# First four feature tiles of a mixture-of-experts layer in plain fp32, with three weight low parts moved to VectorE

## The chip, the cores and the metric

The kernel runs on one core of one Trainium2 chip. The metric is the device time of one execution in microseconds (us), median of several runs. TensorE is called PE, VectorE DVE, ScalarE ACT, GpSimd POOL and SyncE SP, as the profile does.

## The reference

Three layers run one after the other, all in fp32. An mLSTM layer over 2 batches, 8 heads, 768 steps and head size 40 gives a matrix x of 1536 tokens by 320. A dense mixture of 8 experts with Sinkhorn weights follows, and a top-1 mixture of 8 experts closes the program.

```python
h = np.maximum(x @ w1[e], 0.0)      # 320 -> 1024
ye = h @ w2[e]                      # 1024 -> 320
out += P[:, e:e + 1] * ye           # first mixture, all experts
out[mask] = gate_w[mask, None] * ye # second mixture, tokens of expert e
```

## The kernel before, in words

Tokens are worked in 12 tiles of 128. The tiles alternate between the two batches, so tiles 0 and 1 are the first chunks of both, tiles 2 and 3 the second, and so on. `lead` (line 304) computes attention for tiles 0 and 1 at once; `attn` (line 404) is a generator that does one later tile in some fifteen steps.

A product of two fp32 matrices is mostly done in the one-pass type fp32r. Each operand is split into a high part (ACT copies it to fp32r) and a low part (an engine subtracts the high part from the raw value), and three products are added: high by high, high by low, low by high. Contraction runs over the 320 features of x in three blocks of 128, 128 and 64; the third block holds high and low rows of x side by side, so two products do there. That makes 8 matmuls of 256 columns for one feature tile of 128 and two token tiles (`s1_unit`, line 844, matmuls at line 855). Behind them ACT writes the ReLU's high part `hh` (line 856) and DVE its low part `hl` (line 857). `transpose_x` (line 468) turns a token tile of x and splits it into `xh` and `xl`. `split_chunk` (line 597) splits one raw piece of a weight matrix: ACT casts at line 613, DVE or POOL subtracts at line 619, and then the next raw piece is loaded into the freed one of four buffers (`load_chunk`, line 576). The first expert's w1 comes in three raw pieces, its w2 in three more.

The first mixture is a list of items (line 554): tiles 0 and 1 with expert 0, tiles 2 and 3 with expert 0, then four tiles at a time. An item runs 8 feature tiles (stage 1), then for each token tile four pieces of six matmuls with w2 (stage 2, lines 861 to 863). Two background ticks, numbered u, stand in each feature tile and one behind each stage 2 piece. `bg_early` (line 1578) hangs attention work on them: the tables RT, AT, GT and DT (lines 1569 to 1572) say at which u a tile's decay rows R are made (line 207), its attention starts, and gate and decay chains start. So the order in which every engine sees its work is the order of this program text; each engine takes its queue strictly in that order.

At the end of `lead` the queues stand as follows. PE: values of tiles 0 and 1 (line 262), outer product 0 (line 267), transposes of x 0 (lines 473 and 474), two filler matmuls (line 192), transposes of x 1, outer product 1, then feature tile 0. POOL subtracts the low parts of the first two w1 pieces between its gate steps (lines 366 and 382), DVE that of the third (line 388). DVE also normalises tiles 0 and 1 (lines 272 to 274, 377) and scans the next gate chunk (lines 147 to 164).

Of the kernel before, what the change touches and what calls it, by code (L numbers as in the profile page):

```python
# [12 lines left out]
ALU = mybir.AluOpType  # L13
# [5 lines left out]
def mlstm_moe_moe_kernel(ctx, tc, q, k, v, i_gate, f_gate, o_gate, wg1, w1a, w2a, wg2, w1b, w2b, out):  # L19
# [169 lines left out]
    def keep_warm(n, cols=512):  # L189

        for _ in range(n):
            pe.matmul(warm_p[:, 0:cols], warm[:, 0:128], warm[:, 0:cols], start=True, stop=True)
# [111 lines left out]
    def lead(g1):  # L304
# [58 lines left out]
        for i in range(2):  # L363
            for a in range(2):
                values(pn[i], W[i], i, a)
        low = split_chunk(pool, wait=True)
        low()
        pc = [pst(), None]
# [12 lines left out]
        next(g1)  # L381
        low = split_chunk(pool, wait=True)
        low()
        transpose_x(xs_[0], 0, pst, act)
        next(g1)
        next(g1)
        keep_warm(2)
        low = split_chunk(wait=True)
        transpose_x(xs_[1], 1, ps1, act)
        pc[1] = pst()  # L390
        outer(pc[1], 1)
        low()
        next(g1)
        emit_const1()
# [92 lines left out]


    NBLK = 3
    TPB = NT // NBLK  # L490
# [77 lines left out]
    for n, (_, _, e) in enumerate(ITEMS):  # L568
        if n == 0 or ITEMS[n - 1][2] != e:
            chunks += [(e, "w7", t) for t in range(4)] if seven(n) else [(e, "w1", t) for t in range(3)]  # L570
            chunks += [(e, "w2", t) for t in range(3)]
    raws = {}
    nload = [0]
    nsplit = [0]

    def load_chunk():
# [13 lines left out]
        else:  # L590
            k0, k1 = 3 * t, min(3 * t + 3, NF)
            sp.dma_start(out=r[:, 0:(k1 - k0) * DM].rearrange("p (k d) -> p k d", d=DM),
                         in_=w2a[e, k0 * 128:k1 * 128, :].rearrange("(k p) d -> p k d", p=128))
        raws[n] = r
        nload[0] += 1

    def split_chunk(eng=None, wait=False, hi=None):
# [19 lines left out]

        def low():
            eng.tensor_tensor(out=l, in0=rv, in1=f32(h), op=ALU.subtract)  # L619
            load_chunk()  # L620
        if wait:
# [254 lines left out]
    def moe1(bg):  # L876
# [44 lines left out]
        for n, (t0, nt, e) in enumerate(ITEMS):  # L921
# [21 lines left out]
            else:  # L943
                assert not left_over
                for ft in range(NF):
                    s1_unit(t0, nt, ft, lambda: bg(n, 2 * ft))
                    if newe and (ft < 3 if n < EARLY - 2 else ft in (0, 2, 4)) or n == 0 and ft in (2, 4, 6):
                        split_chunk()
                    if sums is not None and ft > 3:
                        next(sums, None)  # L950
                        next(sums, None)
                    bg(n, 2 * ft + 1)
# [595 lines left out]
    with tc.manual_schedule():  # L1548
# [19 lines left out]

        RT = {3: 2, 6: 3, 17: 4, 27: 5, 37: 6, 47: 7, 55: 8, 63: 9, 71: 10, 79: 11}
        AT = {5: 2, 8: 3, 20: 4, 30: 5, 40: 6, 50: 7, 58: 8, 66: 9, 74: 10, 82: 11}  # L1570
        GT = {6: 2, 26: 3, 43: 4, 59: 5}
        DT = {5: 1, 20: 2, 36: 3, 54: 4, 70: 5}
        OT = {10: 2, 25: 4, 43: 6, 60: 8, 76: 10}
# [141 lines left out]
```

## Time and profile before

| what | value |
|---|---|
| median of 3 runs | 959.27 us (958.46 to 960.22) |
| profiled execution | 958.19 us, span 956.5 us |
| PE busy | 927.4 us, 97% of the span |
| DVE busy | 628.3 us, 66% |
| ACT busy | 442.2 us, 46% |
| POOL busy | 257.5 us, 27% |
| mean granted PE clock | 0.991 of full |

The span is the part of the profiled execution between its first and last recorded work. An engine's busy time is the union of its instructions; an idle gap carries the name of what ended it. A row of the timeline gives start, duration, engine, source line and operation, and in square brackets the idle time ahead of it with its releaser. In a view that merges instructions, a duration is that of the whole group. Lines are those of the kernel before. An fp32 matmul shows as two records in the trace, an fp32r matmul as one.

### The profile page before, as it was taken

Reading aid. Unit: us, or ns where it says so; the run is one execution under the profiler, and the core shown is the slowest. Engines: PE = TensorE matmul, PEld = TensorE weight load, DVE = VectorE, ACT = ScalarE, POOL = GpSimd, SP = SyncE. Lnnn points to the kernel's source line nnn. Section 1 sums busy time; section 2 is a strip of 40 time slices with the busy share of each in tenths; the row PEclk is TensorE's granted clock in tenths of the full one; section 3 lists DMA queues with packets and bytes.
Section 4 is the critical chain, followed back from the end, with each engine's and each line's share of the span. In section 5 each row is a group of like instructions: output and inputs, shape, how many; then the busy total and the mean of one; then the engine's idle time right before and its main releaser. Section 6 shows DMA issues by size and latency. Waiting matters only on the chain.

```text
span 956.5 us, 15330 instructions
## 1 busy us (share of the span) xinstructions
PE 927.4 (97%) x5714; PEld 833.7 (87%) x5714; DVE 628.3 (66%) x1325; ACT 442.2 (46%) x790; POOL 257.5 (27%) x271
## 2 busy tenths in 40 slices
PE   8999999999999999999999999999999999899995
PEld 5888888888999998999998889999988987678995
DVE  8767865667766877474856748484536469864772
ACT  4545635343445565352535436253332135565672
POOL 6313321001006341415051231402221102325411
PEclk9999999999999999999999999999999999999998
DMA  9824430323234103021210203022280034677540
GB/s 194 190 43 94 112 92 23 100 77 110 83 96 133 57 1 116 17 77 56 77 56 25 92 17 107 26 77 65 68 320 29 19 93 137 206 226 209 160 119 19
DMA packets 93711, 91.28 MB, mean 95 GB/s; under 512 B 54845, under 2 KB 82495, under 8 KB 93632
## 3 DMA queue, kind: packets, MB, share of 16 engines
q1 hardware_dynamic: 91424, 83.50, 30.8%
q0 software_dynamic: 2208, 6.75, 2.2%
q8 instruction: 47, 0.77, 0.3%
q14 instruction: 32, 0.26, 0.1%
HBM read 86.29 MB, written 4.76 MB: 95 GB/s over the span
## 4 chain that ended last, share of the span: by engine, by line
PE 84%; DVE 8%; DMA 2%; ACT 2%; issue 2%; POOL 1%; SPq 0%; POOLq 0%; DVEq 0%; ACTq 0%
PE a L750 17%; PE s L855 12%; PE s L861 8%; PE s L863 8%; PE s L862 8%; PE s L1414 3%; PE a L861 3%; PE a L863 3%; PE a L862 3%; PE s L750 3%; PE a L262 2%; PE s L1352 2%; PE a L252 1%; PE s L1387 1%; PE s L1397 1%
## 5 line engine op out<-in xcount | busy, mean ns | idle before, releaser
L861 PE MATMUL s<-w2h,hh 128*128 128x320 f32 x544 | 171.5, 315 | 0.0
L863 PE MATMUL s<-w2h,hl 128*128 128x320 f32 x544 | 168.2, 309 | 0.0
L862 PE MATMUL s<-w2l,hh 128*128 128x320 f32 x544 | 168.0, 309 | 0.0
L855 PE MATMUL s<-xh,w 128*128 128x512 f32 (+1 forms) x528 | 147.7, 379 | 2.3 <-DVE hl L857 1.7
L855 PEld LDWEIGHTS s<-xh,w 128*128 128x128 f32 x528 | 96.7, 191 | 22.7 <-DVE hl L857 4.1
L619 POOL TENSOR_TENSOR w2l<-raw,w2h 128x960 fp32r<-128x960 f32 (+1 forms) x24 | 50.1, 2098 | 228.8 <-ACT w2h L613 228.6
L861 PEld LDWEIGHTS s<-w2h,hh 128*128 128x128 f32 x544 | 102.3, 188 | 2.0
L862 PEld LDWEIGHTS s<-w2l,hh 128*128 128x128 f32 x544 | 102.4, 188 | 1.6
L863 PEld LDWEIGHTS s<-w2h,hl 128*128 128x128 f32 x544 | 102.1, 188 | 0.1
L856 ACT ACTIVATE hh<-s 128x512 fp32r<-128x512 f32 (+1 forms) x88 | 49.2, 559 | 107.2 <-PE s L855 107.2
L857 DVE SCALAR_TENSOR_TENSOR hl<-s,hh 128x512 fp32r<-128x512 f32 (+1 forms) x88 | 56.3, 640 | 58.5 <-ACT hh L856 58.3
L750 PE MATMUL a<-th,w 128*128 128x512 f32 (+1 forms) x224 | 80.5, 366 | 0.0
L750 PE MATMUL a<-ts,wx 96*128 96x512 f32 (+1 forms) x192 | 70.7, 368 | 0.9 <-DVE wx L732 0.9
L855 PE MATMUL s<-xl,w 128*128 128x512 f32 (+1 forms) x176 | 67.7, 385 | 1.7 <-DVE xl L483 1.7
L861 PE MATMUL a<-w2h,hh 128*128 128x320 f32 x224 | 69.3, 309 | 0.0
L863 PE MATMUL a<-w2h,hl 128*128 128x320 f32 x224 | 69.2, 309 | 0.0
L862 PE MATMUL a<-w2l,hh 128*128 128x320 f32 x224 | 69.1, 309 | 0.0
L889 DVE SCALAR_TENSOR_TENSOR acc<-s,probs,acc 128x320 f32<-128x320 f32 x68 | 37.3, 548 | 41.2 <-PE s L863 40.8
L777 DVE SCALAR_TENSOR_TENSOR hl<-s,hh 128x512 fp32r<-128x512 f32 (+1 forms) x64 | 39.6, 619 | 30.0 <-ACT hh L773 30.0
L785 ACT COPY pu<-a 128x512 f32<-128x512 f32 (+1 forms) x32 | 17.1, 534 | 87.9 <-PE a L750 82.5
L773 ACT ACTIVATE hh<-a 128x512 fp32r<-128x512 f32 (+1 forms) x64 | 35.0, 547 | 36.9 <-DVE a L780 34.3
L777 DVE SCALAR_TENSOR_TENSOR hl<-a,hh 128x512 fp32r<-128x512 f32 (+1 forms) x64 | 39.9, 623 | 15.1 <-ACT hh L773 12.4
(377 smaller groups left out, 2192.0 us busy)
## 6 DMA issues: line engine op xcount, KB each, us to landing
raw<-in_moe_w_dram SPq DMA_DIRECT2D x30, 512.0 KB, 3.8
raw<-in_moe_w_dram SPq DMA_DIRECT2D x30, 480.0 KB, 3.6
raw<-in_moe_w_dram SPq DMA_DIRECT2D x39, 320.0 KB, 4.3
raw<-in_moe_w_dram SPq DMA_DIRECT2D x40, 256.0 KB, 4.3
wr<-in_moe_w_dram SPq DMA_DIRECT2D x8, 1024.0 KB, 13.7
w2raw<-in_moe_w_dram SPq DMA_DIRECT2D x12, 640.0 KB, 4.1
raw<-in_moe_w_dram SPq DMA_DIRECT2D x42, 128.0 KB, 2.6
q<-in_q_dram SPq DMA_DIRECT2D x12, 160.0 KB, 3.6
```

The costliest lines, as they stand in the source:

```text
L619: eng.tensor_tensor(out=l, in0=rv, in1=f32(h), op=ALU.subtract)
L750: pe.matmul(bank, w, x, start=(first and n == 0), stop=(n == 3), skip_group_check=True)
L773: act.activation(out=hh[:, f, c], in_=p, func=AF.Relu)
L777: dve.scalar_tensor_tensor(out=hl[:, f, c], in0=p, scalar=0.0, in1=f32(hh[:, f, c]), op0=ALU.max, op1=ALU.subtract)
L855: pe.matmul(p, w[:, k, fs], x_[:, k, cols], start=(m == 0), stop=(m == len(mm) - 1))
L856: act.activation(out=hh[:, ft, 0:n], in_=p, func=AF.Relu)
L857: dve.scalar_tensor_tensor(out=hl[:, ft, 0:n], in0=p, scalar=0.0, in1=f32(hh[:, ft, 0:n]), op0=ALU.max, op1=ALU.subtract)
L861: pe.matmul(p[:, 0:DM], hh[:, f, c], w2h[:, w[n], :], start=(first and n == 0), stop=False)
L862: pe.matmul(p[:, 0:DM], hh[:, f, c], w2l[:, w[n], :], start=False, stop=False)
L863: pe.matmul(p[:, 0:DM], hl[:, f, c], w2h[:, w[n], :], start=False, stop=(last and n == len(cuts) - 1))
L889: dve.scalar_tensor_tensor(out=acc[:, tt, 0:DM], in0=p[:, 0:DM], scalar=probs[:, tt, e:e + 1], in1=acc[:, tt, 0:DM], op0=ALU.mult, op1=ALU ...
L1414: pe.matmul(p, a[:, k, fs], b[:, k, xs], start=(k == 0 and n == 0), stop=(k == 2 and n == 1))
```

## The change

The first four feature tiles of the first item (`plain_unit`) multiply the raw fp32 pieces of w1 with an unsplit fp32 copy of x, `xf`, in three plain fp32 matmuls of 256 columns each. `turn_x` only transposes x and copies it to `xf` on ACT; `split_x` makes `xh` and `xl` for both tiles behind feature tile 0. The low parts of all three w1 pieces are subtracted on DVE: two at the end of `lead`, the third behind feature tile 1. The raw pieces are read until feature tile 3, so the next three loads are issued behind it. The splits of the three w2 pieces move from feature tiles 2, 4, 6 to 4, 6, 7. In the background tables the rows R of tiles 2 and 3 move from u 3 and 6 to 5 and 7, their attention from 5 and 8 to 7 and 9, and one gate and one decay chain by two.

```diff
-        low = split_chunk(pool, wait=True)
-        low()
+        lows = [split_chunk(wait=True) for _ in range(2)]
         pc = [pst(), None]
         outer(pc[0], 0)
...
-        low = split_chunk(pool, wait=True)
-        low()
-        transpose_x(xs_[0], 0, pst, act)
+        turn_x(xs_[0], 0, pst)
+        keep_warm(2)
+        turn_x(xs_[1], 1, ps1)
+        pc[1] = pst()
+        outer(pc[1], 1)
+        lows.append(split_chunk(wait=True))
+        lows[0](False)
+        lows[1](False)
         next(g1)
         next(g1)
-        keep_warm(2)
-        low = split_chunk(wait=True)
-        transpose_x(xs_[1], 1, ps1, act)
-        pc[1] = pst()
-        outer(pc[1], 1)
-        low()
-        next(g1)
+        steps.extend([split_x, lambda: lows[2](False)])
         emit_const1()
...
+    xf = scr[:, 0:3 * 2 * L].rearrange("p (a t) -> p a t", t=2 * L)
+    steps = []
+    def turn_x(x, slot, ps):
+        px = ps()
+        for t in range(2):
+            pe.transpose(px[:, t * L:(t + 1) * L], x[:, t * L:(t + 1) * L], ident)
+        pe.transpose(px[0:64, 2 * L:3 * L], x[:, 256:DM], ident)
+        cols = slice(slot * L, (slot + 1) * L)
+        pv = px[:, 0:3 * L].rearrange("p (a t) -> p a t", t=L)
+        act.copy(out=xf[:, 0:2, cols], in_=pv[:, 0:2, :])
+        act.copy(out=xf[0:64, 2, cols], in_=pv[0:64, 2, :])
+    def split_x():
+        c = slice(0, 2 * L)
+        act.copy(out=xh[0][:, 0:2, c], in_=xf[:, 0:2])
+        act.copy(out=xh[0][0:64, 2, c], in_=xf[0:64, 2])
+        dve.tensor_tensor(out=xl[0][:, :, c], in0=xf[:, 0:2], in1=f32(xh[0][:, 0:2, c]), op=ALU.subtract)
+        dve.tensor_tensor(out=xh[0][64:128, 2, c], in0=xf[0:64, 2], in1=f32(xh[0][0:64, 2, c]), op=ALU.subtract)
+    def plain_unit(ft, w, mid):
+        p = ps1()[:, 0:2 * L]
+        for k in range(3):
+            r = slice(0, 128 if k < 2 else 64)
+            pe.matmul(p, w[k][r, ft * 128:(ft + 1) * 128], xf[r, k], start=(k == 0), stop=(k == 2))
+            if k == 0:
+                mid()
+        act.activation(out=hh[:, ft, 0:2 * L], in_=p, func=AF.Relu)
+        dve.scalar_tensor_tensor(out=hl[:, ft, 0:2 * L], in0=p, scalar=0.0, in1=f32(hh[:, ft, 0:2 * L]), op0=ALU.max, op1=ALU.subtract)
+        if steps:
+            steps.pop(0)()
+        if ft == PLAIN - 1:
+            for _ in range(3):
+                load_chunk()
...
-                    s1_unit(t0, nt, ft, lambda: bg(n, 2 * ft))
-                    if newe and (ft < 3 if n < EARLY - 2 else ft in (0, 2, 4)) or n == 0 and ft in (2, 4, 6):
+                    if n == 0 and ft < PLAIN:
+                        plain_unit(ft, first_raws, lambda: bg(n, 2 * ft))
+                    else:
+                        s1_unit(t0, nt, ft, lambda: bg(n, 2 * ft))
+                    if newe and (ft < 3 if n < EARLY - 2 else ft in (0, 2, 4)) or n == 0 and ft in (4, 6, 7):
                         split_chunk()
...
-        RT = {3: 2, 6: 3, 17: 4, 27: 5, 37: 6, 47: 7, 55: 8, 63: 9, 71: 10, 79: 11}
-        AT = {5: 2, 8: 3, 20: 4, 30: 5, 40: 6, 50: 7, 58: 8, 66: 9, 74: 10, 82: 11}
-        GT = {6: 2, 26: 3, 43: 4, 59: 5}
-        DT = {5: 1, 20: 2, 36: 3, 54: 4, 70: 5}
+        RT = {5: 2, 7: 3, 17: 4, 27: 5, 37: 6, 47: 7, 55: 8, 63: 9, 71: 10, 79: 11}
+        AT = {7: 2, 9: 3, 20: 4, 30: 5, 40: 6, 50: 7, 58: 8, 66: 9, 74: 10, 82: 11}
+        GT = {8: 2, 26: 3, 43: 4, 59: 5}
+        DT = {7: 1, 20: 2, 36: 3, 54: 4, 70: 5}
```

With the change, the low part stands at line 659, the plain matmuls at 514, hl of the plain feature tiles at 518, stage 1 at 896 to 898, stage 2 at 902 to 904, and the decay matmuls of `attn` at 412.

The first place is PE's queue from the end of `lead` into the item. In the names, s_384 and s_373 are the banks of x 1, s_414 and s_401 that of feature tile 0, w_81 is w1, and acc holds `xf` (its other end holds the gate chains). Before:

```order
L474 MATMUL s_384<-ident,x 64x128
L267 MATMUL a<-v_99,ku_97 128x82 x4
L855 MATMUL s_414<-xh_65,w_81 128x256
L855 MATMUL s_414<-xl_68,w_81 128x256
L855 MATMUL s_414<-xh_65,w_81 128x256 x2
L855 MATMUL s_414<-xl_68,w_81 128x256
L855 MATMUL s_414<-xh_65,w_81 128x256 x3
```

Two more feature tiles of the same form follow there, and then the two decay matmuls of tile 2 (line 414). The same place with the change:

```order
L495 MATMUL s_373<-ident,x 64x128
L267 MATMUL a<-v_99,ku_97 128x82 x4
L514 MATMUL s_401<-acc,raw 128x256 x3
L514 MATMUL s_416<-acc,raw 128x256 x3
L514 MATMUL s_423<-acc,raw 128x256 x3
L514 MATMUL s_435<-acc,raw 128x256 x3
L412 MATMUL a<-R,gl__109 128x512 x2
L896 MATMUL s_469<-xh_65,w_81 128x256
```

Four feature tiles now stand ahead of the decay matmuls instead of three, and none of them reads a split operand.

The second place is DVE's queue from the next gate chunk to the rows R of tile 2. Before:

```order
L153 TENSOR_TENSOR acc<-acc 16x128
L155 SCALAR_TENSOR_TENSOR acc<-msk,acc 16x128
L483 TENSOR_TENSOR xl_68<-s_384,xh_65 128x2x128
L484 TENSOR_TENSOR xh_65<-s_384,xh_65 64x128
L619 TENSOR_TENSOR w_81<-raw,w_81 128x1024
L157 CAST gx<-acc 16x128
L162 TENSOR_TENSOR gx<-acc,gx 16x128
L857 SCALAR_TENSOR_TENSOR hl<-s_414,hh 128x256
L164 TENSOR_TENSOR gl__109<-acc,gl__109 16x128
L857 SCALAR_TENSOR_TENSOR hl<-s_428,hh 128x256
L207 TENSOR_TENSOR R<-gx,mask 128x512 x2
```

With the change (one more hl, of s_423, and then R follow the last row):

```order
L659 TENSOR_TENSOR w_81<-raw,w_81 128x1024 x2
L153 TENSOR_TENSOR acc<-acc 16x128
L155 SCALAR_TENSOR_TENSOR acc<-msk,acc 16x128
L157 CAST gx<-acc 16x128
L518 SCALAR_TENSOR_TENSOR hl<-s_401,hh 128x256
L506 TENSOR_TENSOR xl_68<-acc,xh_65 128x2x256
L507 TENSOR_TENSOR xh_65<-acc,xh_65 64x256
L162 TENSOR_TENSOR gx<-acc,gx 16x128
L164 TENSOR_TENSOR gl__109<-acc,gl__109 16x128
L518 SCALAR_TENSOR_TENSOR hl<-s_416,hh 128x256
L659 TENSOR_TENSOR w_81<-raw,w_81 128x1024
```

The split of x moved behind the first hl and is done once for both tiles; two low parts of w1 joined this queue.

The third place is DVE's queue at the end of stage 1, where the scores of tiles 2 and 3 are weighed (line 257, each twice) and the last w2 pieces are split. Before:

```order
L857 SCALAR_TENSOR_TENSOR hl<-s_507,hh 128x256
L619 TENSOR_TENSOR w2l<-raw,w2h 128x960
L153 TENSOR_TENSOR acc<-acc 16x128
L155 SCALAR_TENSOR_TENSOR acc<-msk,acc 16x128
L857 SCALAR_TENSOR_TENSOR hl<-s_568,hh 128x256
L257 TENSOR_TENSOR W<-a,W 128x4x128 x2
L157 CAST gx<-acc 16x128
L857 SCALAR_TENSOR_TENSOR hl<-s_603,hh 128x256
L619 TENSOR_TENSOR w2l<-raw,w2h 128x640
```

With the change:

```order
L898 SCALAR_TENSOR_TENSOR hl<-s_519,hh 128x256
L153 TENSOR_TENSOR acc<-acc 16x128
L155 SCALAR_TENSOR_TENSOR acc<-msk,acc 16x128
L898 SCALAR_TENSOR_TENSOR hl<-s_561,hh 128x256
L659 TENSOR_TENSOR w2l<-raw,w2h 128x960
L257 TENSOR_TENSOR W<-a,W 128x4x128 x2
L157 CAST gx<-acc 16x128
L257 TENSOR_TENSOR W<-a,W 128x4x128 x2
L898 SCALAR_TENSOR_TENSOR hl<-s_597,hh 128x256
```

The weighing of tile 2 now stands behind hl of feature tile 6 (s_561) and the low part of the second w2 piece; before, it stood behind hl of feature tile 5 (s_568). On PE the values of tile 2, which read the weighed scores, moved from feature tile 7 to between the first pieces of stage 2.

## Rows read from the trace of the kernel before

**Rows 1.** The page: PE's busy time, and PE over 40 slices of the span.
```profile
PE 927.4 (97%) x5714; PEld 833.7 (87%) x5714; DVE 628.3 (66%) x1325; ACT 442.2 (46%) x790; POOL 257.5 (27%) x271
...
PE   8999999999999999999999999999999999899995
```

**Rows 2.** The timeline of PE, 17 to 30 us: start, duration, instructions, idle time ahead.
```profile
17.89 0.66 PE L473 MATMUL a<-ident,x 128*128 128x128 f32 x2 [1.10 <-DVE num L374]
...
23.55 0.39 PE L855 MATMUL s<-xl,w 128*128 128x256 f32 x1 [1.73 <-DVE xl L483]
...
25.13 0.80 PE L855 MATMUL s<-xh,w 128*128 128x256 f32 x2 [0.59 <-DVE w L619]
...
29.04 1.01 PE L414 MATMUL a<-R,gl__109 128*128 128x512 f32 x2 [0.31 <-DVE R L207]
```

**Rows 3.** The timeline of DVE, 14 to 30 us.
```profile
14.77 2.01 DVE L272 SCALAR_TENSOR_TENSOR den<-num 128x8 f32<-128x8 f32 x1
...
18.14 0.17 DVE L272 SCALAR_TENSOR_TENSOR den<-num 128x8 f32<-128x8 f32 x1
...
18.78 0.49 DVE L377 TENSOR_TENSOR x<-num,den 128x320 f32<-128x320 f32 x1
...
19.90 0.41 DVE L483 TENSOR_TENSOR xl<-a,xh 128x256 fp32r<-128x256 f32 x1
...
20.64 2.10 DVE L153 TENSOR_TENSOR acc<-acc 16x128 f32<-16x128 f32 x1
...
23.85 1.23 DVE L619 TENSOR_TENSOR w<-raw,w 128x1024 fp32r<-128x1024 f32 x1
24.99 0.21 DVE L157 CAST gx<-acc 16x128 fp32r<-16x128 f32 x1
...
28.21 1.28 DVE L207 TENSOR_TENSOR R<-gx,mask 128x512 fp32r<-128x512 f32 x2
```

**Rows 4.** The timeline of POOL, 14 to 23 us.
```profile
14.39 2.36 POOL L619 TENSOR_TENSOR w<-raw,w 128x1024 fp32r<-128x1024 f32 x1
...
20.25 2.34 POOL L619 TENSOR_TENSOR w<-raw,w 128x1024 fp32r<-128x1024 f32 x1
```

**Rows 5.** Stretches of 2 us: length, engines' busy time, granted PE clock, DMA.
```profile
17.00:19.00 2.00, 1.11 (x5) 0.74 (x5) 1.84 (x8) 0.20 (x1) 0.00 (x0) 0.71 0.99 168
...
25.00:27.00 2.00, 1.87 (x8) 1.88 (x9) 1.19 (x5) 0.38 (x1) 0.71 (x3) 0.50 0.99 222
```

**Rows 6.** The timeline of PE at 807 us: plain fp32 matmuls and what follows.
```profile
807.32 2.40 PE L1397 MATMUL s<-w2raw,hraw 128*128 128x320 f32 x8
809.57 0.66 PE L1365 MATMUL a<-ident,acc 128*128 128x128 f32 x4
```

**Rows 7.** The chain that ended last, 25 to 64 us: start, share of the chain in us, work.
```profile
25.13 3.61 PE s L855 x17
...
29.14 0.88 ACT w2h L613
30.03 0.51 ACT W L230
30.56 0.63 ACT W L237
...
41.98 0.82 PE a L262 x8
...
63.54 1.41 PE s L855 x12
```

**Rows 8.** The timeline of PE, 39 to 45 us: scores of tile 3, start of stage 2.
```profile
39.21 1.16 PE L252 MATMUL a<-qT,kT 40*128 40x128 f32 x16 [0.20 <-ACT kT L423]
...
43.99 0.39 PE L861 MATMUL s<-w2h,hh 128*128 128x320 f32 x1
...
44.95 1.02 PE L445 MATMUL a<-cbd,qT 128*128 128x82 f32 x8
```

**Rows 9.** The page: DMA issues, size of one, median us to landing.
```profile
raw<-in_moe_w_dram SPq DMA_DIRECT2D x30, 480.0 KB, 3.6
```

More of the change, by code (lines that the diff above doesn't have):

```diff
@@ L572, in mlstm_moe_moe_kernel @@
     raws = {}
+    first_raws = []
+    PLAIN = 4
     nload = [0]
@@ L594, in load_chunk @@
         raws[n] = r
+        if n < 3:
+            first_raws.append(r)
         nload[0] += 1
@@ L616, in split_chunk, with low @@
         nsplit[0] += 1
-        def low():
+        def low(more=True):
             eng.tensor_tensor(out=l, in0=rv, in1=f32(h), op=ALU.subtract)
-            load_chunk()
+            if more:
+                load_chunk()
         if wait:
```

## The prediction

> **What bounds the kernel now.** I read the page first. PE is busy for 97% of the span, and its 40 slices show nine tenths or more everywhere but in the first and in those near the end [rows 1]. So time won early is kept only if PE is what waits early and what is full afterwards; both hold. The timeline of PE names the early waits: 1.10 us ahead of the transposes of x 0, 1.73 us for a low part of x, 0.59 us for a low part of w1, 0.31 us for R [rows 2]. All four end with DVE. The timeline of DVE then shows why DVE is late. A tiny operation on 8 columns, L272, takes 2.01 us for tile 0 and 0.17 us for tile 1; L153, on 16 partitions, takes 2.10 us [rows 3]. Beside each, POOL subtracts a low part of w1, from 14.39 to 16.75 and from 20.25 to 22.59 [rows 4], and DVE's operations end at 16.78 and 22.74. DVE was held until POOL was done. The granted clock shows a second cost: 0.71 in the stretch that holds the first wait and 0.50 two stretches after the longest, which is the lower level, 1.2 of 2.4 GHz [rows 5].
>
> The Trainium skill, "SBUF — State Buffer", section "SBUF: two separate sides", says that VectorE and GpSimd share a pair of SBUF ports under an exclusive lock, held for a whole instruction. The two stretched operations agree. The rule also speaks against the change: a subtraction with two SBUF inputs on DVE would hold POOL. POOL's share of the next gate chunk would then finish later and DVE's L164 wait for it, by my estimate 0.3 us; the sum below would come out 0.3 us later.
>
> **POOL's low parts leave.** DVE's L272 falls from 2.01 to 0.17, so x 0 and x 1 come 1.84 us earlier [rows 3]. The start of x 1's normalising multiplication goes from 18.78 to 16.94, and the point behind x 1, L147 and L150 from 19.90 to 18.06. The 1.95 us that L153 spent under the second POOL subtraction go too [rows 3, 4].
>
> **DVE's new queue to the rows R of tile 2.** From 18.06: two low parts at 1.14 each (start of L619 to start of L157 [rows 3]) to 20.34. Three small gate steps at 0.3, taken between the 0.17 and 0.49 of small operations [rows 3], to 21.24. hl of feature tile 0 at 0.41, the width of L483, to 21.65. The split of x for both tiles: one operation of 512 columns and one of 256. The trace has none of this exact form; 0.41 for 256 columns and 1.14 for 1024 bound the wide one, and half of 1.28 for the same 512 columns is nearest [rows 3]. I take 0.64 and 0.41, to 22.70, with bounds of half a microsecond on either side. Two gate steps to 23.30, hl to 23.71, the third low part to 24.85, hl to 25.26, the first half of R at 0.64 to 25.90. The decay matmuls of tile 2 start at 26.0, against 29.04 before [rows 2].
>
> **PE beside it.** Outer product 0 ends at 16.79 (17.89 less the wait of 1.10 [rows 2]). x 0 is there by then, so the 1.10 us wait goes. x 1, ready at 17.43 (18.78 + 0.49 - 1.84 [rows 3]), is reached at about 17.5. Its transposes (two of the three took 0.66 at the lower clock [rows 2]), ACT's copies at some 0.5 and the semaphores put the first plain matmul near 19; outer product 1 runs meanwhile. A plain matmul of 320 columns is two records, eight of which take 809.57 - 807.32 = 2.25 us, or 0.28 each [rows 6]. Scaled to 256 columns that is 0.225, and six records make 1.35 us a feature tile. Twelve fp32r matmuls of 256 columns hold the chain for 1.41 us at full clock, so the eight of a feature tile take 0.94; seventeen hold it for 3.61 at the lower level, so eight take 1.70 [rows 7]. Bounds for the plain tile are 0.70 (six records at the fp32r price) and 1.69 (the 320-column price unscaled), and twice 1.35 at the lower clock. Four tiles add 4 x (1.35 - 0.94) = 1.64 us of PE work, but they end at 19 + 5.4 = 24.4, or at 25.1 since the third and fourth wait for banks that hl frees at 21.65 and 23.71. Both lie ahead of 26.0, so this work is hidden behind DVE. If the clock halves, it isn't (rival 1).
>
> The Trainium skill, "FP8 and Floating Point Precision", section "TensorE Precision Notes", counts four passes for true FP32. Twelve passes against eight would cost half as much again, an estimate of 1.41 us a tile. On a PE that was the bound here, that rule alone would make the kernel 1.9 us slower; DVE's queue is why I don't forecast it.
>
> **From the decays to stage 2.** At 26.0 one more feature tile is behind us than at 29.04. Next ACT sets the pace, as the chain shows it did before [rows 7]. It starts 0.5 us behind the first decay, at 26.5. Up to kT of tile 3 it does four ReLUs at 0.53 and four exponentials at 0.63 (starts and shares in [rows 7]), three copies of the same 512 columns at 0.5, two hh at 0.3 (estimated from the 512-column price), one w2 cast at 0.89, small ones for 0.2, and kT itself at 0.6: 2.1 + 2.5 + 1.5 + 0.6 + 0.9 + 0.2 + 0.6 = 8.4, to 34.9. Scores of tile 3 start there, against 39.21 [rows 8]. They take 1.1, the second half of feature tile 6 ends at 36.5, feature tile 7 at 37.4.
>
> **The wait that is new.** PE then does one stage 2 piece, 0.96 (43.99 to 44.95 [rows 8]), to 38.4, and needs the weighed scores of tile 2. On DVE these now stand behind hl of feature tile 6 (36.5, 0.5 for ACT's hh, 0.41: 37.4) and the low part of the second w2 piece. Its cast on ACT runs from 37.0 to 37.9, the low part, at 1.1 like L619, to 39.0. Half of the weighing, 512 columns at R's 0.64, ends at 39.6. So PE waits 1.2 us. Values, piece, values at 0.82 [rows 7], 0.96, 0.82 follow to 42.2. Before, stage 2 began at 43.99 with the values done; two pieces later is 45.9. The gain is 45.9 - 42.2 = 3.7 us; I write 3.6, for the semaphores between so many short steps.
>
> **What costs nothing.** The three raw loads now leave at about 25 us, behind feature tile 3. A load lands 3.6 us after its issue in the median [rows 9], and the cast that needs the first is due at 37; late loads would hold that cast and, with it, the weighing. Attention of tiles 2 and 3 starts 2 and 1 ticks later. The transposes of x 3 stand at tick 22 and the item that reads them starts at tick 24. One piece (0.96), a set of scores (1.1) and a turn lie between, against two copies and two subtractions at 0.3 to 0.5; that cover is thin. SP's queue carries the same loads.
>
> **Sum.** The profiled execution took 958.19 us, its span 956.5 and 1.7 around it; 958.19 - 3.6 = 954.6. The median of the runs is 1.08 above that execution, so I predict 959.27 - 3.6 = 955.7.
>
> **Rivals.** A difference within 0.2%, 1.9 us, can't be told from no change.
>
> 1. *The lower clock comes back* (0.17). The waits that remain on PE, above all the new 1.2 us, resemble the 1.10 and 1.73 us beside which the clock stood at the lower level [rows 2, 5]. Against it: the plain tiles keep PE occupied from 17 to 25 us. If half of the 3.4 us of pieces and values, or a tile and a half of plain work past DVE's slack, run at the lower level, 1.7 to 2 us of the gain go: 957.5.
> 2. *The weighing is not late* (0.15). If ACT's cast and DVE's low part come sooner than I sum, the 1.2 us wait is gone: 954.5.
> 3. *Moving POOL's low parts frees nothing* (0.12). If L272 is slow for another reason, x 0 and x 1 stay 1.84 us late and so does the queue behind them: gain 1.8, 957.5. Against it: both long operations end within 0.15 us of POOL's [rows 3, 4].
> 4. *PE becomes the bound at the lower clock* (0.06, slower). From 16.8 to the common point PE has about 20 us of work at full clock (plain tiles 5.4, fp32r tiles 3.8, pieces 1.9, values 1.6, scores 2.2, decays 1.8, some 3.3 of turns, outer products and fillers) and, in my sum, 42.2 - 16.8 - 20 = 5.4 us of waits. Each microsecond of work at the lower level costs another one. The first 5.4 fill the waits, the next 3.7 the gain. So beyond 9 us of work at 1.2 GHz it is slower, and all 20 would end at 56.8 instead of 45.9: 970. For it: plain tiles at 2.7 us each would end at 30, behind DVE. Against it: the lower level was seen only near waits of over 1 us.
>
> **How the numbers follow.** The forecast holds with 0.50. Its own spread, from the split of x and the ACT estimates, is about 1.3 us each way. The range 953.9 to 958.2 takes in rivals 2, 1 and 3 and leaves out rival 4 and the tails, some 0.2. Faster by over 1.9 us: nearly all of the forecast, rival 2, and a third of rivals 1 and 3, so 0.72. Slower by over 1.9: 0.06. The rest, 0.22, is the same.
>
> **What would show it.** L272 at about 0.2 us twice, transposes of x 0 without a wait, plain records of 0.22 us spacing, decays of tile 2 near 26.0 ended by R, scores of tile 3 near 35, a wait of 1.2 us ended by the weighing near 39, and the later program shifted as a whole. The prediction is wrong if the decays come after 28, or if the shift of 3 to 4 us at stage 2 shrinks before the first unit of the second item.

## The result: slower by 1.0%

| | before | changed |
|---|---|---|
| median of 6 runs each | 959.37 us (958.46 to 960.22) | 968.34 us (966.00 to 971.21) |
| ratio of the times | | 1.0097, 95% interval 1.0075 to 1.0118 |
| profiled execution | 958.19 us, span 956.5 | 967.01 us, span 965.3 |
| mean granted PE clock | 0.991 | 0.986 |

The forecast was 955.7, with a range of 953.9 to 958.2. The page shows a PE that is busy 7.5 us longer with eight matmul records fewer, and is still full nearly everywhere [rows 1]. So the loss is in what PE's work costs, more than in waits.

```profile
PE 934.9 (97%) x5706; PEld 839.1 (87%) x5706; DVE 629.5 (65%) x1325; ACT 442.6 (46%) x792; POOL 254.4 (26%) x269
...
PE   9899999999999899999999999999999999899995
```

Up to 43 us the timeline of PE reads much as forecast (start, duration, work, idle time ahead and its releaser):

```profile
16.71 0.38 PE L494 MATMUL a<-ident,x 128*128 128x128 f32 x2
...
18.95 5.07 PE L514 MATMUL s<-acc,raw 128*128 128x256 f32 x18
24.74 1.76 PE L514 MATMUL s<-acc,raw 128*128 128x256 f32 x6 [0.73 <-DVE hl L518]
...
26.89 1.30 PE L412 MATMUL a<-R,gl__109 128*128 128x512 f32 x2 [0.40 <-DVE R L207]
...
36.70 1.16 PE L252 MATMUL a<-qT,kT 40*128 40x128 f32 x16 [0.20 <-ACT kT L421]
...
39.31 0.31 PE L902 MATMUL s<-w2h,hh 128*128 128x320 f32 x1
...
41.69 1.08 PE L262 MATMUL a<-v,W 128*128 128x41 f32 x8 [1.33 <-DVE W L257]
...
43.57 2.83 PE L262 MATMUL a<-v,W 128*128 128x41 f32 x16
...
63.34 1.16 PE L252 MATMUL a<-qT,kT 40*128 40x128 f32 x16 [0.44 <-DVE cbd L289]
```

The waits of 1.10, 1.73 and 0.59 us are gone [rows 2], the decays of tile 2 start at 26.89 instead of 29.04, and stage 2 at 39.31 instead of 43.99 [rows 8]. Then a wait of 1.33 us comes for the weighed scores. From the values at 43.57 on, 16 matmuls take 2.83 us where 8 take 1.08 two rows above. The scores of tile 4, a point that both kernels pass, come at 63.34; before:

```profile
59.50 1.16 PE L252 MATMUL a<-qT,kT 40*128 40x128 f32 x16
```

So a lead of 4.68 us at the start of stage 2 (part of it only order: values of tile 2 now stand behind it) has become 3.84 us of lag 24 us later. The stretches name the cause (length, PE busy, granted PE clock, DMA share, GB/s). After:

```profile
28.00:32.00 4.00, 4.00 (x24) 0.68 0.91 249
...
44.00:48.00 4.00, 4.00 (x20) 0.53 1.09 225
48.00:52.00 4.00, 4.00 (x20) 0.50 0.02 9
52.00:56.00 4.00, 4.00 (x25) 0.69 0.26 43
...
316.00:320.00 4.00, 1.23 (x5) 0.66 0.41 130
320.00:324.00 4.00, 4.00 (x19) 0.50 0.22 58
```

PE is busy without a break from 44 to 56 us, at the lower level, 1.2 of 2.4 GHz, for most of it: (1 - 0.53) x 4 + (1 - 0.50) x 4 + (1 - 0.69) x 4 is 5.1 us of full-speed work lost. The kernel before has 1.00 in the three stretches from 44 to 56 and in the two at 316 and 320, of which two are shown:

```profile
44.00:48.00 4.00, 4.00 (x34) 1.00 0.95 215
...
316.00:320.00 4.00, 4.00 (x36) 1.00 0.49 154
```

The rows at 316 and 320 of the changed kernel are a second loss, far from the change, where seven products replace eight for the first time (item 7; `s1_seven`, fed by `make_sums`, whose sums of weights DVE splits into `wx`). The lag of the same matmuls grows there from 4.09 us (at 303 us of before) to 8.90 (at 323); the two executions differ by 967.01 - 958.19 = 8.82. The same four operations on DVE and POOL, and PE's product behind them. Before:

```profile
308.51 1.22 DVE L728 TENSOR_TENSOR wx<-sums,w 128x1024 fp32r<-128x1024 f32 x1
309.76 2.42 DVE L732 TENSOR_TENSOR wx<-sums,wx 32x1536 fp32r<-32x1536 f32 x1
...
308.79 1.79 POOL L615 CAST w2h<-raw 128x960 fp32r<-128x960 f32 x1 [3.71 <-PE a L863]
310.66 3.65 POOL L619 TENSOR_TENSOR w2l<-raw,w2h 128x960 fp32r<-128x960 f32 x1
...
312.24 0.39 PE L750 MATMUL a<-ts,wx 96*128 96x256 f32 x1 [0.89 <-DVE wx L732]
```

After:

```profile
313.02 2.01 DVE L769 TENSOR_TENSOR wx<-sums,w 128x1024 fp32r<-128x1024 f32 x1
315.06 3.65 DVE L773 TENSOR_TENSOR wx<-sums,wx 32x1536 fp32r<-32x1536 f32 x1
...
312.88 1.07 POOL L655 CAST w2h<-raw 128x960 fp32r<-128x960 f32 x1 [3.29 <-PE a L904]
314.03 3.07 POOL L659 TENSOR_TENSOR w2l<-raw,w2h 128x960 fp32r<-128x960 f32 x1
...
318.77 0.58 PE L791 MATMUL a<-ts,wx 96*128 96x256 f32 x1 [3.30 <-DVE wx L773]
```

Before, DVE's first operation begins 0.28 us ahead of POOL's cast, and DVE's two take 3.67 us in all. After, POOL begins 0.14 us ahead, and the same two take 5.69 us while POOL's subtraction shortens from 3.65 to 3.07. PE's wait grows from 0.89 to 3.30, and the clock falls within it: full up to 316 us, 0.66 in the next stretch, while PE's product starts at 318.77. POOL's cast waits for PE to free a buffer. DVE's operations wait for ACT (2.27 us for a cast at 307 us), ACT for POOL's sums, and these for a raw load (2.15 us at 302.6). By these releasers, which goes first depends on how PE stands to the loads, by some tenths of a microsecond; no run varies that alone.

The other profiles agree. Where POOL went first in item 7 (the changed kernel, and the first, third and fourth kernel and the repeat of the change below) PE waited 3.25 to 3.30 us there; in every profile with DVE first it waited 0.93 us or less.

### The profile page after: what moved, and what is told of

Read it like the earlier page. It is cut to its first block, busy times and chain, and to the rows that moved or that the text cites. A ratio compares the mean times of both kernels' runs of the same rounds, so it can differ in the third digit from the quotient of the medians.

```text
span 965.3 us, 15316 instructions
## 1 busy us (share of the span) xinstructions
PE 934.9 (97%) x5706; PEld 839.1 (87%) x5706; DVE 629.5 (65%) x1325; ACT 442.6 (46%) x792; POOL 254.4 (26%) x269
## 4 chain that ended last, share of the span: by engine, by line
PE 87%; DVE 5%; DMA 2%; ACT 2%; issue 2%; POOL 1%; POOLq 0%; SPq 0%; DVEq 0%; ACTq 0%
PE a L791 17%; PE s L896 12%; PE s L902 8%; PE s L904 8%; PE s L903 8%; PE a L902 3%; PE a L904 3%; PE a L903 3%; PE s L1458 3%; PE s L791 3%; PE a L262 2%; PE s L1396 2%; PE a L252 1%; PE s L1431 1%; PE a L443 1%
## 5 line engine op out<-in xcount | busy, mean ns | idle before, releaser
L896 PE MATMUL s<-xh,w 128*128 128x512 f32 (+1 forms) x504 | 142.7, 382 | 1.7 <-DVE hl L898 1.6
L896 PEld LDWEIGHTS s<-xh,w 128*128 128x128 f32 x504 | 92.7, 190 | 22.0 <-DVE hl L898 4.5
L896 PE MATMUL s<-xl,w 128*128 128x512 f32 (+1 forms) x168 | 65.3, 389 | 0.0
L818 DVE SCALAR_TENSOR_TENSOR hl<-s,hh 128x512 fp32r<-128x512 f32 (+1 forms) x64 | 39.6, 618 | 30.0 <-ACT hh L814 30.0
```

The costliest lines, as they stand in the source:

```text
L818: dve.scalar_tensor_tensor(out=hl[:, f, c], in0=p, scalar=0.0, in1=f32(hh[:, f, c]), op0=ALU.max, op1=ALU.subtract)
L896: pe.matmul(p, w[:, k, fs], x_[:, k, cols], start=(m == 0), stop=(m == len(mm) - 1))
```

## Experiments

Each run is compared with runs of the kernel before on the same chip (957.6 to 965.3 us in all, medians 959.15 to 960.97). The chips differ from run to run, so runs on different chips are compared by these ratios. "Lead" is 59.50 less the start of the scores of tile 4 in the profile of that run.

**What brings the first loss.** Four kernels on one chip. The first takes the wait away by order: the split of w2's second piece goes behind the weighing.

```diff
-... or n == 0 and ft in (4, 6, 7):
+... or n == 0 and ft in (4, 7):
                         split_chunk()
...
                     bg(n, 2 * ft + 1)
+                    if n == 0 and ft == 6:
+                        split_chunk()
```

> One move against the changed kernel: the split of the second w2 piece is emitted behind the second tick of feature tile 6, so DVE weighs the scores of tile 2 ahead of that low part. Theory A (the 1.33 us wait for the weighed scores, in front of a run of values with 41 columns, lets PE's clock fall to 1.2 GHz from 44 to 54 us): the wait falls below 0.4 us, the clock stays at 1.00 in 44 to 54, the second item starts near 56 instead of 64; time 958 to 960 if the second loss near 316 us stays, 954 to 956 if it goes too. Rival B (the clock falls because of the plain fp32 tiles or the denser run of small matmuls, whatever the wait): the clock still falls near 44, only the 1.33 us are won: 966 to 967.

Measured: 962.29 us, ratio 1.0023 (1.0002 to 1.0045). No wait for weighed scores, full clock from 20 to 64 us, lead 2.54. The loss at item 7 stayed, with POOL's cast 0.40 us ahead of DVE (lead 2.17 at 303 us, lag 2.02 at 323). The time lies between the two forecasts; the clock from 44 to 54 is what theory A said.

The second keeps the late weighing and fills the wait with six filler matmuls at tick 16.

```diff
         def bg_early(u):
+            if u == 16:
+                keep_warm(6)
```

> One addition to the changed kernel: six filler matmuls of 512 columns (1.3 us at full clock) behind the first piece of stage 2, where PE waits for the weighed scores. Nothing gets earlier by it. Theory A: clock at 1.00 from 44 to 54, second item near 57, time 959 to 961 with the second loss near 316 us, 955 to 957 without. Rival B: low clock as before, 967 to 970.

Measured: 959.89 us, ratio 0.9984 (0.9971 to 0.9997). Full clock from 20 to 64 and a lead of 1.19, which went in a low stretch from 67 to 71. In item 7 DVE went first, and nothing was lost there.

The third is the kernel before with the first two low parts on DVE, without plain tiles; the fourth the change with the old tables RT, AT, GT and DT.

```diff
-        low = split_chunk(pool, wait=True)
-        low()
+        low0 = split_chunk(wait=True)
...
-        low = split_chunk(pool, wait=True)
-        low()
+        low1 = split_chunk(wait=True)
+        low0()
+        low1()
```

> The kernel before with one part of the change alone: the low parts of the first two w1 pieces on DVE instead of POOL, no plain tiles, old tables. If POOL's two subtractions are what held DVE's L272 and L153: both fall to 0.2 to 0.3 us, x 0 comes 1.8 us earlier, DVE pays 2.3 us for the two low parts, the third low part of w1 ends 1.4 us earlier, time 957.5 to 958.5. If they are not: L272 stays at 2 us, DVE is 2.3 us later, time 961 to 962.

Measured: 959.60 us, ratio 0.9982 (0.9972 to 0.9993), lead 0.98. L272 took 0.17 us twice and L153 0.28, so POOL's subtractions were what held them; the time missed the 957.5 to 958.5 expected. In its profile POOL went first in item 7 by 0.05 us, which hides the lead there.

```diff
-        RT = {5: 2, 7: 3, ...
-        AT = {7: 2, 9: 3, ...
+        RT = {3: 2, 6: 3, ...
+        AT = {5: 2, 8: 3, ...
```

> The changed kernel with the old background tables: rows R of tiles 2 and 3 at ticks 3 and 6, attention at 5 and 8, gate and decay chains as before. DVE then weighs tile 2 ahead of the second low part of w2 and the values of tile 2 return into stage 1. Theory A: no wait of over 0.5 us ahead of the values, no long low stretch, second item near 57, time 955 to 960. Rival B (plain tiles cost the clock): low clock from about 44 again, time 965 or more.

Measured: 962.75 us, ratio 1.0014 (0.9995 to 1.0033). The wait moved: 2.56 us ahead of the decays of tile 2, none for the weighing, and full clock from 32 to 64; lead 1.48. The time lies between the two forecasts, with the loss at item 7 in it (POOL 0.40 us ahead).

Three of these four have the plain tiles, and in the profile of none was the clock low between 44 and 64 us. So plain tiles alone do not bring the long low stretch; it was absent where the wait ahead of it was absent or filled.

A wait is not all that brings the lower clock, though. In the profiles of the first three kernels it also came from about 16 to 19 us, where PE had not waited by more than 0.1 us since 1.3 us; it was then in values and outer products of 41 and 82 columns. In that of the third (no plain tiles) it came again at 67 to 71 us, with PE fully busy and no wait over 0.1 us for 12 us ahead:

```profile
64.00:68.00 4.00, 4.00 (x34) 0.93 0.00 0
68.00:72.00 4.00, 4.00 (x24) 0.65 0.00 0
```

**The second loss.** One column is copied on POOL ahead of its first cast in item 7. It reads the last part of `wx` that DVE writes, so POOL cannot go first.

```diff
+                        if n == SEVEN and j == 0:
+                            pool.tensor_copy(odd[64:96], f32(sx["wx"][64:96, 8, HF - 1:HF]))
                         split_chunk(hi=None if wide else pool)
```

> The changed kernel with one extra copy of a single column on POOL ahead of its first cast in item 7, which reads the last part that DVE writes of wx; so POOL's cast and subtraction can't start ahead of DVE's two operations on wx there. Theory: the second loss, at 312 to 324 us, comes from the order of DVE and POOL at that place (POOL's cast 0.14 us ahead of DVE's product in the changed kernel, 0.28 us behind it before). Then the two operations on wx take 3.6 us instead of 5.7, PE's wait there falls from 3.30 us to about 1, the clock stays at 1.0 from 316 to 324, and 4 to 5 us come back: 963 to 965, still slower than before by the 3.9 us of the first loss. Rival: the loss there is what a late raw load costs anyway, whichever engine goes first; then PE still waits about 3 us and the time stays at 967 to 969.

Measured: 960.46 us (958.26 to 968.42), ratio 1.0022 (0.9995 to 1.0050). In its timelines DVE takes 1.22 and 1.75 us, and PE waits 0.93:

```profile
309.10 1.22 DVE L770 TENSOR_TENSOR wx<-sums,w 128x1024 fp32r<-128x1024 f32 x1
310.35 1.75 DVE L774 TENSOR_TENSOR wx<-sums,wx 32x1536 fp32r<-32x1536 f32 x1
...
312.17 0.18 POOL L979 COPY odd<-wx 32x1 f32<-32x1 f32 x1 [6.50 <-DVE wx L774]
...
312.16 0.38 PE L792 MATMUL a<-ts,wx 96*128 96x256 f32 x1 [0.93 <-DVE wx L774]
```

The median fell further than the 963 to 965 expected. The one profile, of the fastest of the ten runs, shows the first loss small: the lower clock came from 35 to 42 us, PE reached the weighing late enough not to wait, and the scores of tile 4 stood 0.30 us ahead of before. That most of the ten went this way is likely, not shown; two took 966.95 and 968.42.

> The kernel before with the same extra copy on POOL ahead of its first cast in item 7. Theory: DVE goes first there in most of its runs, so the median moves by less than 1 us either way (959.5 to 961.5) and the highest run comes down from the 964 to 965 that some of its runs took. Rival: the extra copy makes POOL late (it now starts 3 us later, behind both operations on wx), its low part of w2 comes late to PE, and the kernel is 2 to 3 us slower.

Measured: 958.78 us (957.76 to 960.60), ratio 0.9994 (0.9983 to 1.0004), while the kernel before reached 964.69 beside it. The long runs went, as expected; the median hardly moved.

The same edit with the fillers of the second kernel, and with the weighing first:

> The changed kernel with six filler matmuls in the wait for the weighed scores and with DVE first in item 7: both losses addressed. Theory: the first loss goes as with the fillers alone, and the runs in which POOL went first are helped too; the median falls below the 959.9 of the fillers alone, to 957.5 to 959.5, 1.5 to 3 us below the kernel before on this chip, with a narrower spread. Rival: the fillers' run already had DVE first, so nothing changes: 960.

Measured: 958.80 us, ratio 0.9995 (0.9976 to 1.0014), not better than the fillers alone (0.9984): the rival holds. In its profile the clock was low from 35 to 42 us, ahead of the fillers, and the scores of tile 4 stood 0.81 us behind before.

> The changed kernel with the weighing of tile 2 ahead of the split of w2's second piece, and with DVE first in item 7. Theory: its 2.2 us lead at 303 us then outlasts item 7, where 4.2 us were lost; the median falls from 962.3 to 957.5 to 959, about 2.5 us below the kernel before. Rival: the lead is only time by which PE reaches the same late loads earlier, so it is lost at item 7 as a longer wait whichever engine goes first: 960.5 to 962.5.

Measured: 957.01 us, ratio 0.9973 (0.9958 to 0.9988); the lead of 2.53 us outlasts item 7. Beside 1.0023 without the copy, the order at item 7 was worth 0.5%.

The change as it is, on another chip, beside two more:

> The changed kernel itself once more, beside the next two, so that their differences are read on one chip. Theory: both losses are in it, the low clock behind the wait for the weighed scores in most runs and POOL ahead of DVE in item 7 in nearly all, so it comes out 4 to 9 us over the kernel before, and 4 us or more over the version with DVE first alone. Rival: the 9 us were a matter of that one chip, and here it is within 2 us of the kernel before.

Measured: 965.21 us (962.54 to 966.84), ratio 1.0051 (1.0031 to 1.0072). Slower again, by half as much. In its profile POOL went first in item 7 (0.41 us ahead) and 4.2 us went there (the same matmuls of both traces, at 303 and at 323 us), while the first loss was missing: low clock from 35 to 42 and a lead of 0.30. That profile is of the fastest of the six runs; what the others lost early is not seen.

The next makes PE's wait longer, with three operations on DVE ahead of the weighing.

```diff
+        if i == 2:
+            for _ in range(3):
+                dve.tensor_scalar_max(out=junk, in0=W[:, 0:4, :].rearrange("s h t -> s (h t)"), scalar1=0.0)
         weigh(W, sc)
```

> The version with DVE first in item 7 and the weighing still late (960.5 us, runs from 958.3 to 968.4, where the kernel before took 959.2), with three more operations of 512 columns on DVE ahead of the weighing of tile 2, whose results nothing reads. They make PE wait 1 to 2 us longer there. Theory: the low clock follows that wait, so it now comes in nearly all runs: the median goes to 964 to 969, far more than the added wait. Rival: the time is only shifted by the wait, 1 to 2 us over the version without the three operations: 961.5 to 962.5, with the same two kinds of runs.

Measured: 966.06 us (964.42 to 969.47), ratio 1.0066 (1.0040 to 1.0091). The three operations took 1.34 us together and all six runs were long: 0.0044 more than without them is 4.2 us. The two ratios come from different chips, and their intervals touch (1.0040 here, 1.0050 there). In the profile the clock was low from 36 to 43 us, as without the three operations, and this time PE still had to wait for the weighing. Behind the wait of 1.40 us the clock fell as in the change:

```profile
44.44 1.08 PE L264 MATMUL a<-v,W 128*128 128x41 f32 x8 [1.40 <-DVE W L259]
```

```profile
44.00:48.00 4.00, 3.56 (x23) 0.78 0.92 197
48.00:52.00 4.00, 4.00 (x19) 0.50 0.40 123
52.00:56.00 4.00, 4.00 (x31) 0.87 0.00 0
```

**Why the low stretch moves.** The version with weighing and DVE first, run once more:

> The version with the weighing first and DVE first in item 7, no fillers, once more on the chip of the run above, so that the two compare. Its ratio to the kernel before was 0.9973 with an interval of 0.9958 to 0.9988; if waits of 0.4 to 0.7 us decide the low clock it is 1 to 3 us slower than the version with ten fillers, if not the two are within 1 us.

Measured: 959.51 us (956.61 to 963.39), ratio 0.9987 (0.9969 to 1.0005), 3.9 us slower than the version with ten fillers (below) on the same chip, where 1 to 3 were expected. This is one program with two profiles. The first run, and the second:

```profile
28.00:32.00 4.00, 4.00 (x26) 0.71 1.04 300
...
36.00:40.00 4.00, 3.80 (x38) 1.00 0.95 168
```

```profile
28.00:32.00 4.00, 3.97 (x31) 1.00 0.99 194
...
36.00:40.00 4.00, 4.00 (x26) 0.50 1.00 235
40.00:44.00 4.00, 4.00 (x20) 0.50 0.29 49
```

At 28 to 32 the low stretch costs little (lead 2.53), at 35 to 45 it costs 4.1 us more (scores of tile 4 at 61.04). Shorter waits lie ahead of both places: 0.73 to 0.88 and 0.40 us at 25 and 27, in the second run also 0.44 and 0.66 at 32 and 34. The same two early waits were followed by the low stretch in one run and not in the other. Fillers had gone into the first two before this repeat, and went into all four beside it.

```diff
         p = ps1()[:, 0:2 * L]
+        if ft == 3:
+            keep_warm(3)
         for k in range(3):
...
             if u in AT:
+                if u == 7:
+                    keep_warm(2)
```

> The version with the weighing first and DVE first in item 7 (957.0 us where the kernel before took 959.2), with three filler matmuls in the 0.73 us wait ahead of the fourth plain tile and two in the 0.40 us wait ahead of the decays of tile 2. Theory that PE's waits are what the low clock follows: with these two filled the stretch at the lower level from 27 to 31 us is gone, the point behind it comes up to 1.5 us sooner, and the median is 0.5 to 1.5 us better, 2.7 to 3.7 us below the kernel before. Rival: that stretch lies in the shadow of ACT and DVE, so nothing is won and five fillers of 0.21 us cost up to 0.5 us: 1.7 to 2.2 us below the kernel before.

Measured: 957.97 us (954.69 to 961.72), ratio 0.9971 (0.9952 to 0.9989). The stretch at 27 to 31 was gone, but in the profile the clock was low from 35 to 42 instead. The median is 2.6 us below the kernel before, between what the rival (1.7 to 2.2) and the theory (2.7 to 3.7) expected; the interval takes in both. Its runs go by their mean clock: the four at 0.993 to 0.996 took 954.7 to 955.8, the eight at 0.988 to 0.990 took 957.1 to 961.7.

```diff
+        if c0 == 1:
+            keep_warm(2)
         p = pst()
...
         sc = [ps(), ps()]
+        if i == 2:
+            keep_warm(3)
         scores(sc, qT, kT)
```

> The version with the weighing first, DVE first in item 7 and fillers in the waits at 24 and 26 us (0.9971 of the kernel before), with two more filler matmuls ahead of the transposes of the decays that feed tile 3 (PE waits 0.42 us there at 31.9) and three ahead of the scores of tile 2 (0.66 us at 33.5). Theory: the stretch at the lower level that came at 34 to 41 us in its profile follows those two waits, so it goes in all or nearly all runs: the lowest time stays at 954 to 955, the median falls from 958 to 954.5 to 956, about 0.995 of the kernel before, and the spread of 7 us shrinks. Rival: the low stretch comes in some runs whatever PE waits for there; then the median stays at 0.997 of the kernel before, with the same spread.

Measured: 955.57 us (954.45 to 957.56), ratio 0.9954 (0.9937 to 0.9971). Median and lowest time are what the theory said. Full clock from 16 to 64 us and a lead of 2.69, but low later:

```profile
64.00:68.00 4.00, 4.00 (x24) 0.64 0.00 0
68.00:72.00 4.00, 4.00 (x19) 0.51 0.02 4
```

Two more fillers went into each of the last two waits before it, 0.40 us at 53 and 0.44 at 57.

```diff
+            if i == 4 and src is qs[j]:
+                keep_warm(2, to=ps1())
...
-        if i == 2:
-            keep_warm(3)
+        if i == 2 or i == 4:
+            keep_warm(3 if i == 2 else 2, to=None if i == 2 else ps1())
```

> The version with weighing first, DVE first in item 7 and ten fillers (0.9954 of the kernel before), with two more filler matmuls in each of the two waits that remain before 60 us, 0.40 us at 53.0 and 0.44 us at 56.8. In the profile of the version with ten fillers the clock was at the lower level from about 64 to 71 us, and a lead of 2.7 us went to nothing there. Theory: that stretch follows the two waits as the earlier ones did, so it goes; the median falls by 1 to 2 us more, to 0.993 to 0.9945 of the kernel before. Rival: that stretch comes from what PE does behind 57 us, where it has no wait at all (scores, decays and router columns on a few rows), and then the time stays at 0.995 to 0.9955.

Measured: 955.38 us (952.58 to 956.19), ratio 0.9952 (0.9933 to 0.9971). In the profile the clock is full from 16 to 72 us and the lead 2.97; its own time is 954.59. The median is what the rival expected: four of six runs still have a mean clock of 0.992 or 0.993 and take 955.2 to 956.2, the other two 0.997. This is the best version found, 0.5% faster than the kernel before; from the version with ten fillers the times do not tell it apart.

The last run asks what fillers do without the change: the kernel before, DVE first in item 7, and fillers in its three early waits.

```diff
         low()
+        keep_warm(5)
         transpose_x(xs_[0], 0, pst, act)
...
+    first_unit = {1: 8, 7: 2}
...
+            if first_unit and m in first_unit:
+                keep_warm(first_unit.pop(m))
             pe.matmul(p, w[:, k, fs], ...
```

> The kernel before with DVE first in item 7 and with filler matmuls in its three early waits: five ahead of the transposes of x 0 (1.10 us), eight in the 1.73 us wait for the low part of x, two in the 0.59 us wait for the low part of w1. Theory: in the kernel before, DVE's queue sets the pace up to 29 us, and the lower clock from 17 to 29 us lies in its shadow; so the clock is at the full level there and the time moves by less than 1 us, 0.9985 to 1.0005 of the kernel before. Rival: the low clock of the kernel before is what made its early part slow, and the fillers alone give what the change was meant to give: 0.996 or less.

Measured: 956.01 us (954.82 to 957.64), ratio 0.9961 (0.9946 to 0.9976): what the rival expected by time, and against my theory. The profile speaks for neither alone:

```profile
24.00:28.00 4.00, 3.82 (x25) 1.00 1.01 215
```

```profile
23.90 0.39 PE L861 MATMUL s<-xl,w 128*128 128x256 f32 x1 [0.86 <-DVE xl L485]
...
58.78 1.16 PE L253 MATMUL a<-qT,kT 40*128 40x128 f32 x16
```

The clock is full early, yet PE still waits for DVE and the lead is 0.72 us; another 1.2 is won at item 7, where PE did not wait. That is 1.9 us at 324 us of the profile against 3.1 in the medians. The rest has not been placed.

## Why the prediction was wrong

- **POOL's low parts leave: right.** L272 takes 0.17 us twice, and L153 0.53 instead of 2.10 [rows 3].

```profile
14.86 0.17 DVE L272 SCALAR_TENSOR_TENSOR den<-num 128x8 f32<-128x8 f32 x1
...
16.46 0.17 DVE L272 SCALAR_TENSOR_TENSOR den<-num 128x8 f32<-128x8 f32 x1
...
18.22 2.34 DVE L659 TENSOR_TENSOR w<-raw,w 128x1024 fp32r<-128x1024 f32 x2
20.49 0.53 DVE L153 TENSOR_TENSOR acc<-acc 16x128 f32<-16x128 f32 x1
...
39.87 1.16 DVE L659 TENSOR_TENSOR w2l<-raw,w2h 128x960 fp32r<-128x960 f32 x1 [0.46 <-ACT w2h L653]
40.95 1.28 DVE L257 TENSOR_TENSOR W<-a,W 128x512 f32<-128x512 f32 x2
```

POOL's L151, on 16 partitions, took 2.82 us beside DVE's two low parts, and L164 then waited 0.23 us for POOL. The rule of the Trainium skill, "SBUF — State Buffer", section "SBUF: two separate sides", agrees in that L151 ended only behind DVE's pair (20.87 and 20.56); I had estimated 0.3.

- **The plain tile: the mis-sized term, hidden.** 18 records in 5.07 us are 1.69 us a tile: the upper bound, not the 1.35 taken. The scaling by columns was right. In the tile that starts at 20.57, records inside the 128-row blocks start 0.22 us apart (20.89, 21.11, 21.32), and the 320-column records of [rows 6] 0.27 apart. What the sum left out is the change between blocks of 128 and of 64 rows: the next weight load starts there only after 0.33 us in which its queue is idle, and the four steps beside the changes take 0.31 to 0.32 us (20.57 to 20.89, 21.32 to 21.63 to 21.95, and to 22.26, the next tile). Four steps longer by some 0.1 make the 0.39 over six equal steps, 1.30.

```profile
20.57 0.73 PEld L514 LDWEIGHTS s<-acc,raw 128*128 128x128 f32 x4 [0.33 <-issue]
21.63 0.29 PEld L514 LDWEIGHTS s<-acc,raw 64*128 64x128 f32 x2 [0.33 <-issue]
```

No run isolates the number of rows as the reason. DVE ended the wait that followed, so this cost little. The Trainium skill, "FP8 and Floating Point Precision", section "TensorE Precision Notes", counts four passes, from which I had estimated 1.41 us a tile. Inside a block the trace nearly agrees: two records of 0.22 are 0.43 us a matmul, 3.7 times the 0.12 of an fp32r one.
- **The sum to stage 2: right in kind, 2 us late.** Decays at 26.89 instead of 26.0, scores of tile 3 at 36.70 instead of 34.9 (ACT began 0.9 us late, at 27.44, and took 0.9 longer; PE's clock stood at 0.68 from 28 to 32, and its part in that is not separated), the weighing at 41.69 instead of 39.6. At full clock the two sets of values and the piece between them would have ended at 41.69 + 0.82 + 0.96 + 0.82 = 44.3, a gain of 1.6 and not 3.6 against 45.9. The wait itself was found, in its place and nearly its size: 1.33 for 1.2.
- **The step that failed: that the new wait costs only itself.** Rival 1 had the mechanism, the lower clock that comes back, and priced it at 1.7 to 2 us, as half of 3.4 us of pieces and values. The low stretch lasted until about 54.5 us, and 5.1 us of work were lost in it: 45.9 - 44.3 = 1.6 of gain less 5.1 is 3.5 of lag, where 3.84 were measured. Rival 4 came nearest (970, with a chance of 0.06): I held against it that the lower level was seen only near waits of over 1 us, and then forecast such a wait. The profiles tie this stretch to the wait. Of the thirteen with plain tiles, the two with a wait of 1.3 to 1.4 us for the weighing (the change, and the lengthened wait) have the clock low behind it, and none of the other eleven has it low between 45 and 64 us. The times lean the same way, less firmly. With DVE first, the runs with the weighing first took 0.9973 and, repeated, 0.9987 (up to 1.0005), those with it late 1.0022 (from 0.9995), and those with the wait lengthened 1.0066. That every low stretch needs a wait is not so: see the third kernel above.
- **The second step that failed: "the later program shifted as a whole".** It held to 0.25 us from 62 to 303 us. At item 7, 0.4 us in the order of two engines cost another 4.8 us, 2.4 of them before PE's product and the rest behind it, at the lower clock. Nothing in the prediction looked there. The version with POOL held back shows it.
- **Rivals 2 and 3** fell with the rows: the weighing was late, and L272 and L153 were freed. Of the marks named in advance, the shift at stage 2 that shrinks before the second item is the one that came.
- **Cover.** Raw loads and the transposes of x 3 cost nothing that the timelines show. The later ticks of attention are not free of cost: with the old tables there was no wait for the weighing, but one of 2.56 us ahead of the decays.
- **What the change is worth.** With the clock held up in both, the scores of tile 4 come at 56.53 with the change and at 58.78 without: 2.25 us, in which the shorter queue on DVE and the fillers in two later waits of the first version are not separated. The times, 0.9952 and 0.9961 with intervals that overlap, do not separate the two.

Open stays what begins a low stretch where PE has not waited, and what ends one: PE was busy without a break from 44 to 56 us of the changed kernel, in matmuls of 41 to 320 columns, and the clock stayed low. Open too is why one program meets it at different places from run to run.

## What to carry to other kernels

A wait that moves from a place where another engine is the bound to a place where PE is the bound can cost more than its length: a low clock that follows is then paid in full (1.33 us of wait, 5.1 us of work here). So price a new wait on PE with the low stretches that the profile of before already shows, wherever they happen to be free now. Fill such waits with filler matmuls, or reorder the engine that ends them, before a change is judged. A shift in time is not neutral for later code where two engines that hold each other up are released by different clocks (a buffer freed by PE, a load): fix their order by a dependency.

## What the runs showed of the hardware

- Records of plain fp32 matmuls of 256 columns started 0.22 us apart inside a block of 128 rows, those of 320 columns 0.27. Beside each change between 128 and 64 rows a step took 0.31 to 0.32, with the weight load's queue idle for 0.33 us.
- The lower clock lasted 10 us while PE was fully busy (44 to 54 us). It was also met where PE had not waited by more than 0.1 us for 12 us or longer: near 16 us in three profiles, and at 67 us in the kernel before with its low parts on DVE.
- POOL's cast 0.14 us ahead of DVE's two operations, instead of 0.28 us behind their start, made these 2.0 us longer (5.69 for 3.67). Held back behind both, POOL's cast and subtraction took 0.99 and 2.27 us instead of 1.79 and 3.65.
